# Query weights in two runs of 16 KB to a partition, with a second copy of x to match

## The chip, the cores and the metric

One core of one Trainium2 chip. The metric is device microseconds of one execution.

## The reference

One decode step: a layer norm of x (512 numbers), then two branches that are multiplied. Branch A is attention of 32 heads over the last 4,096 rows of a K and a V cache (64 MB, the bulk of the traffic); its query is `xn @ wq`, with `wq` 512 x 4,096 in bf16 (4 MB). Branch B is a small MLP on the same `xn`.

```
x  = A_x                                     # [1, 1, 512]
xn = layernorm(x)
q  = (xn @ wq) -> 32 heads of 128            # wq: 512 x 4096
s  = softmax(q k^T * Dh**-0.5) v @ wo        # k, v: the last 4096 of 32768 rows, 32 heads
x1 = xn + shifted(gelu(layernorm(xn) @ w1)) @ w2     # one row only, so the shifted rows are zero
g  = silu(x1 + gelu(layernorm(x1) @ w3) @ w4)
out = x + s * g
```

## The kernel before

x lies over the partitions four numbers to each (`x[4p + c]` in partition p), and the weights' rows lie the same way, so partition p of the query weights is one run of 4 rows, 32 KB, in memory. All large loads go through the sync engine's queue, in program order; the two small loads of x through the scalar engine's.

```python
    small.tile([P, 64], BF16, name="pad")                 # unused: places the tiles after it
    ...
    def load(dst, src):
        return tc.keep_in_program_order(nc.sync.dma_start(out=dst, in_=src))

    x_bf = small.tile([P, KC], BF16, name="x_bf")         # KC = 4: 128 pieces of 8 B
    nc.scalar.dma_start(out=x_bf[:], in_=A_x.rearrange("a b (p c) -> p (a b c)", p=P))
    x_row = small.tile([P, P], BF16, name="x_row")        # 4 rows of 256 B
    ...
    load(w2_sb[:], ...); load(w3_sb[:], ...); load(w4_sb[...], ...)   # 4096, 11008, 8192, 2048, 1024 B to a partition
    wq_sb = wts.tile([P, KC, HD], BF16, name="wq_sb")
    load(wq_sb[:], A_wq.rearrange("(p c) n -> p c n", p=P))           # 32,768 B to a partition
    ...
    x_f = small.tile([P, KC], FP32, name="x_f")
    nc.vector.tensor_copy(out=x_f[:], in_=x_bf[:])
    xc, negmean, rstd = ln_stats(x_f[:], "x")
    xn_f = small.tile([P, KC], FP32, name="xn_f")
    nc.vector.tensor_scalar(out=xn_f[:], in0=xc[:], scalar1=rstd[:], scalar2=None, op0=ALU.mult)
    xn_bf = small.tile([P, KC], BF16, name="xn_bf")
    nc.vector.tensor_copy(out=xn_bf[:], in_=xn_f[:])
    ...                                                   # the MLP branch, up to bv and g_row
    for h in range(H):
        for c in range(KC):
            nc.tensor.matmul(qT_ps[:, h:h + 1], lhsT=wq_sb[:, c, h * Dh:(h + 1) * Dh],
                             rhs=xn_bf[:, c:c + 1], start=(c == 0), stop=(c == KC - 1))
    ...                                                   # 16 steps of K (VectorE and TensorE) and V (TensorE)
```

K tiles have 6 buffers, V tiles 3, of 16 KB to a partition each; K and V loads are issued as buffers come free.

Of the kernel before, what the change touches and what calls it, by code (L numbers as in the profile page):

```python
# [8 lines left out]
P = 128  # L9
BF16 = mybir.dt.bfloat16  # L10
FP32 = mybir.dt.float32
ACT = mybir.ActivationFunctionType
ALU = mybir.AluOpType
# [16 lines left out]
def kernel(  # L30
# [14 lines left out]
    nc = tc.nc  # L45
# [20 lines left out]
    small = ctx.enter_context(tc.tile_pool(name="small", bufs=1))  # L66
# [3 lines left out]
    ps_o = ctx.enter_context(tc.tile_pool(name="ps_o", bufs=1, space=PSUM))  # L70
    ps_y = ctx.enter_context(tc.tile_pool(name="ps_y", bufs=1, space=PSUM))
    sm_pool = ctx.enter_context(tc.tile_pool(name="sm", bufs=3))
    small.tile([P, 64], BF16, name="pad")
    wts_guard = tc.tile_pool(name="wts", bufs=1)
    wts = wts_guard.__enter__()

    def load(dst, src):
        return tc.keep_in_program_order(nc.sync.dma_start(out=dst, in_=src))  # L78

    x_bf = small.tile([P, KC], BF16, name="x_bf")  # L80
    nc.scalar.dma_start(out=x_bf[:], in_=A_x.rearrange("a b (p c) -> p (a b c)", p=P))
    x_row = small.tile([P, P], BF16, name="x_row")
    nc.gpsimd.memset(x_row[:], 0.0)
    nc.scalar.dma_start(out=x_row[0:P:32, :], in_=A_x.rearrange("a b (j n) -> (a b j) n", j=KC))
# [6 lines left out]
    load(w4_sb[:, 8:10, :], B_w4[8 * P:10 * P, :].rearrange("(p c) n -> p c n", p=P))  # L91
    load(w4_sb[0:96, 10, :], B_w4[10 * P:F, :])
    wq_sb = wts.tile([P, KC, HD], BF16, name="wq_sb")
    load(wq_sb[:], A_wq.rearrange("(p c) n -> p c n", p=P))

    def load_kv(pool, cache, i, cuts=None):
        t = pool.tile([P, CP, Dh], BF16, tag="kv", name="kv")
# [57 lines left out]
    def ln_stats(src_f, tag):  # L155
        ps = ps_misc.tile([P, KC], FP32, tag="misc", name="ln_ps")
        nc.tensor.matmul(ps[:], lhsT=ones_f[:], rhs=src_f, start=True, stop=True)  # L157
        tot = small.tile([P, 1], FP32, name=f"ln_tot_{tag}")
        nc.vector.reduce_sum(out=tot[:], in_=ps[:], axis=AX.X)
        negmean = small.tile([P, 1], FP32, name=f"ln_negmean_{tag}")  # L160
        nc.vector.tensor_scalar(out=negmean[:], in0=tot[:], scalar1=-1.0 / D,
                                scalar2=None, op0=ALU.mult)
        xc = small.tile([P, KC], FP32, name=f"ln_xc_{tag}")
        nc.vector.tensor_scalar(out=xc[:], in0=src_f, scalar1=negmean[:], scalar2=None,
                                op0=ALU.add)
        sq = small.tile([P, KC], FP32, name=f"ln_sq_{tag}")
        nc.vector.tensor_tensor(out=sq[:], in0=xc[:], in1=xc[:], op=ALU.mult)
        ps2 = ps_misc.tile([P, KC], FP32, tag="misc", name="ln_ps2")
        nc.tensor.matmul(ps2[:], lhsT=ones_f[:], rhs=sq[:], start=True, stop=True)
        vtot = small.tile([P, 1], FP32, name=f"ln_vtot_{tag}")  # L170
        nc.vector.reduce_sum(out=vtot[:], in_=ps2[:], axis=AX.X)
        rstd = small.tile([P, 1], FP32, name=f"ln_rstd_{tag}")
        nc.vector.tensor_scalar(out=rstd[:], in0=vtot[:], scalar1=1.0 / D,
                                scalar2=LN_EPS, op0=ALU.mult, op1=ALU.add)
        nc.gpsimd.tensor_tensor(out=rstd[:], in0=rstd[:], in1=neg_half[:], op=ALU.pow)
        return xc, negmean, rstd
# [4 lines left out]
    xc, negmean, rstd = ln_stats(x_f[:], "x")  # L181
    xn_f = small.tile([P, KC], FP32, name="xn_f")
    nc.vector.tensor_scalar(out=xn_f[:], in0=xc[:], scalar1=rstd[:], scalar2=None, op0=ALU.mult)
    xn_bf = small.tile([P, KC], BF16, name="xn_bf")
    nc.vector.tensor_copy(out=xn_bf[:], in_=xn_f[:])



# [3 lines left out]
    for j in range(KC):  # L192
        for c in range(KC):
# [10 lines left out]
                            op0=ALU.add, op1=ALU.mult)  # L204
# [56 lines left out]
    for c in range(2):  # L261
        nc.vector.tensor_copy(
            out=few[:, c, 0:4 * NE].rearrange("p (a b) -> p a b", b=4),
            in_=ident_bf[:, 4 * NE * c:4 * NE * (c + 1)].rearrange("p (b a) -> p a b", b=4))
# [18 lines left out]
                            scalar1=two[:], scalar2=None, op0=ALU.add)  # L283
    md = const.tile([4, 2, 2], FP32, name="md")
    nc.vector.tensor_scalar(out=md[:], in0=ident_f[0:4, 2:4].unsqueeze(1).to_broadcast([4, 2, 2]),
                            scalar1=-1.0, scalar2=1e30, op0=ALU.add, op1=ALU.mult)
# [5 lines left out]
    for r in range(2):  # L292
        nc.vector.tensor_copy(out=pick_f[:, :, r, :],
                              in_=ident_bf[:, 32 * r:32 * r + 8].rearrange("p (i a) -> p i a", a=2))
# [351 lines left out]
```

## Time and profile before

| | |
|---|---|
| three timed executions | 195.66, 195.69, 195.76 us |
| the execution that was profiled | 196.92 us (span 195.1) |
| DMA traffic | 78.84 MB in the sync queue |
| stream | from 1.75 to 190.46 us of the span, never empty after 2.5 us |

The prediction shows the page's slices and the queue table. A packet is one record of a DMA engine moving one run of bytes; "stream" is used here for the run of packets in the sync engine's queue on the 16 DMA engines; as it is never empty, the kernel ends 4.6 us after it does.

### The profile page before, as it was taken

What the parts mean: (1) busy time and instruction counts of PE and PEld (TensorE: products, weight loads), DVE (VectorE), ACT (ScalarE), POOL (GpSimd) and SP (SyncE); (2) the same over time, 40 slices, a digit from 0 to 9 for tenths busy, and PEclk for the clock granted to TensorE, in tenths of its full rate; (3) what the DMA queues carried; (4) which work ended last, traced back from release to release, by engine and by line L of the source; (5) the groups of instructions that cost most, each with busy time, mean ns of one, the idle gap of its engine ahead of it and who ended that gap; (6) DMA issues with size and microseconds to landing.
All of it is one profiled execution on the core that took longest, in us unless ns stands there. A gap on an engine that the chain in (4) does not pass through costs nothing.

```text
span 195.1 us, 4727 instructions
## 1 busy us (share of the span) xinstructions
PE 137.3 (70%) x2108; PEld 105.2 (54%) x2108; DVE 145.2 (74%) x164; ACT 79.0 (40%) x173; POOL 6.3 (3%) x13
## 2 busy tenths in 40 slices
PE   0549779673785899397977957367767897957751
PEld 0434469563784945235967342167656536945640
DVE  0550109999999999999999999079899996982001
ACT  2003019881945742327467053152555018933000
POOL 2110007000000000000000000000000000000000
PEclk9999966967558559759687696965555569675555
DMA  6999999999999999999999999999999999999980
GB/s 200 413 415 410 373 427 423 428 420 430 430 423 430 430 425 427 433 430 430 423 430 430 427 433 427 430 433 430 430 430 427 430 422 432 423 433 420 402 311 4
DMA packets 7052, 79.13 MB, mean 406 GB/s; under 512 B 889, under 2 KB 1753, under 8 KB 2265
## 3 DMA queue, kind: packets, MB, share of 16 engines
q1 hardware_dynamic: 6880, 78.84, 96.1%
q8 instruction: 16, 0.26, 0.5%
q10 hardware_dynamic: 152, 0.00, 0.0%
q14 instruction: 4, 0.02, 0.0%
HBM read 78.84 MB, written 0.00 MB: 404 GB/s over the span
## 4 chain that ended last, share of the span: by engine, by line
DVE 47%; DMA 24%; PE 17%; ACT 5%; issue 4%; SPq 1%; POOL 1%; POOLq 0%
DVE S L315 28%; DVE prod L313 15%; DMA kv<-in_A_v_cache_dram 15%; DMA wo_rows<-in_A_wo_dram 7%; ACT kt L329 4%; PE yr_ps L507 3%; PE oT L442 3%; PE ov L431 3%; DMA x_bf<-in_A_x_dram 2%; PE qT_ps L239 2%; PE hr_ps L223 2%; SPq L78 1%; PE a_ps L212 1%; PE hr_ps L220 1%; DVE m L353 1%
## 5 line engine op out<-in xcount | busy, mean ns | idle before, releaser
L315 DVE TENSOR_REDUCE S<-prod 128x20 f32<-128x2560 bf16 (+1 forms) x32 | 83.8, 2620 | 1.1
L329 ACT COPY kt<-pt 128x1024 bf16<-128x1024 bf16 x54 | 50.9, 1021 | 28.0 <-PE pt L328 28.0
L313 DVE TENSOR_TENSOR prod<-kv,q_bc 128x2560 bf16<-128x2560 bf16 (+1 forms) x32 | 44.3, 1385 | 9.0 <-DMA kv<-in_A_k_cache_dram 6.4
L328 PE MATMUL pt<-ident_bf,kv 128*128 128x128 bf16 x432 | 41.0, 277 | 10.4 <-DMA kv<-in_A_k_cache_dram 8.8
L328 PEld LDWEIGHTS <-kv 128*128 128x128 bf16 x432 | 37.4, 129 | 13.7 <-DMA kv<-in_A_k_cache_dram 10.2
L334 PE MATMUL sT<-qT_bf,kt 128*128 128x2 bf16 x432 | 17.7, 165 | 11.8 <-ACT kt L329 11.2
L442 PE MATMUL oT<-pT,kv 128*128 128x2 bf16 x768 | 22.3, 165 | 4.6 <-DMA kv<-in_A_v_cache_dram 4.6
L442 PEld LDWEIGHTS <-kv 128*128 128x128 bf16 x768 | 21.4, 102 | 6.0 <-DMA kv<-in_A_v_cache_dram 5.9
L334 PEld LDWEIGHTS <-kt 128*128 128x128 bf16 x432 | 15.9, 102 | 14.8 <-ACT kt L329 14.0
L431 PE MATMUL ov<-kv,pT 128*8 128x512 bf16 x64 | 21.9, 517 | 0.0
L431 PEld LDWEIGHTS <-pT 128*8 128x8 bf16 x64 | 6.7, 109 | 13.9 <-issue 11.4
L378 ACT ACTIVATE pT<-S,mb 128x64 bf16<-128x64 f32 x32 | 10.9, 356 | 0.2
L371 PE MATMUL mb_ps<-md,par_t 4*128 4x4 f32 x16 | 3.9, 314 | 9.5 <-DVE md L363 9.5
L374 ACT COPY mb<-mb_ps 128x4 f32<-128x4 f32 x8 | 1.3, 162 | 19.3 <-PE mb_ps L371 19.3
L371 PEld LDWEIGHTS mb_ps<-md,par_t 4*128 4x128 f32 x16 | 3.4, 263 | 10.1 <-issue 8.8
L462 DVE TENSOR_TENSOR o<-oT,rden 128x2 bf16<-128x2 f32 x3 | 0.5, 160 | 11.1 <-PE oT L442 11.1
L466 ACT ACTIVATE o<-oT,rden 128x1 bf16<-128x1 f32 x26 | 4.7, 264 | 6.6 <-PE oT L449 4.7
L226 DVE COPY hr<-hr_ps 1x512 f32<-1x512 f32 x1 | 0.7, 677 | 7.9 <-PE hr_ps L223 7.9
L507 PE MATMUL yr_ps<-wo,ox 128*1 128x512 bf16 x16 | 6.3, 576 | 0.0
L378 ACT ACTIVATION_READ_ACCUMULATOR pT<-S,mb 128x1 f32 x32 | 6.0, 187 | 0.0
L157 PE MATMUL ln_ps<-x_f,ones_f 128*128 128x4 f32 x4 | 1.2, 364 | 6.1 <-DVE x_f L180 5.1
L215 ACT ACTIVATE a_bf<-a_ps 128x10 bf16<-128x10 f32 x1 | 0.2, 180 | 12.4 <-PE a_ps L212 12.4
(116 smaller groups left out, 95.1 us busy)
## 6 DMA issues: line engine op xcount, KB each, us to landing
kv<-in_A_k_cache_dram SPq DMA_DIRECT2D x16, 2048.0 KB, 29.9
kv<-in_A_v_cache_dram SPq DMA_DIRECT2D x15, 2048.0 KB, 26.9
wq_sb<-in_A_wq_dram SPq DMA_DIRECT2D x1, 4096.0 KB, 19.1
wo<-in_A_wo_dram SPq DMA_DIRECT2D x1, 2048.0 KB, 28.2
w_sb<-in_B_w_dram SPq DMA_DIRECT2D x1, 1376.0 KB, 6.7
w_sb<-in_B_w_dram SPq DMA_DIRECT2D x1, 1024.0 KB
wo<-in_A_wo_dram SPq DMA_DIRECT2D x1, 1024.0 KB, 26.8
kv<-in_A_v_cache_dram SPq DMA_DIRECT2D x1, 1024.0 KB
```

Of the source, the lines that this page charges most:

```text
L223: nc.tensor.matmul(hr_ps[:], lhsT=a_bf[0:m, i:i + 1], rhs=w4_sb[0:m, i, :], start=False, stop=(i == len(chunks) - 1))
L313: nc.vector.tensor_tensor(out=prod[:, 0:m, :], in0=kn[:, rows, :], in1=q_bc[:, s:s + 1, :].to_broadcast([P, m, Dh]), op=ALU.mult)
L315: nc.vector.tensor_reduce(out=st[s // 2]["S"][:, s % 2, rows], in_=prod[:, 0:m, :], axis=AX.X, op=ALU.add)
L328: nc.tensor.transpose(pt[:, i, :], kn[:, n + b + i, :], ident_bf[:])
L329: nc.scalar.copy(out=kts[s][:, b:b + w, :], in_=pt[:, 0:w, :])
L334: nc.tensor.matmul(st[s // 2]["sT"][:, s % 2, c, :], lhsT=kt[:, c, :], rhs=qT_bf[:, 2 * s:2 * s + 2], start=True, stop=True)
L371: nc.tensor.matmul(mb_ps[:], lhsT=par_t[:].rearrange("k b a -> k (b a)"), rhs=md[:].rearrange("k r a -> k (r a)"), start=True, stop=True)
L378: nc.scalar.activation(out=s["pT"][:, i // 2, :, i % 2], in_=s["S"][:, i // 2, :], func=ACT.Exp, scale=scale, bias=mb[:, i:i + 1], accum_o ...
L431: nc.tensor.matmul(s["ov"][32 * r:32 * r + 8], lhsT=s["pT"][:, r, c:c + 4, :].rearrange("p i a -> p (i a)"), rhs=v[:, c:c + 4, :], start=F ...
L442: nc.tensor.matmul(s["oT"][:, 2 * r:2 * r + 2], lhsT=v[:, c, :], rhs=s["pT"][:, r, c, :], start=(c == 0), stop=(c == CP - 1))
L466: nc.scalar.mul(o_blk[b][:, c + k:c + k + 1], st[g]["oT"][:, hl + k:hl + k + 1], st[g]["rden"][:, hl + k:hl + k + 1])
L507: nc.tensor.matmul(yr_ps[:], lhsT=ox_blk[i][:, t:t + 1], rhs=wo_blk[i][:, t, :], start=(t == 0), stop=(t == n - 1))
```

## The change

Its intent: runs of 16 KB, the size at which all K and V tiles stream, in place of the slower packets of 32 KB. Row `256 j + 2 p + i` of the query weights now goes to partition p, so x is needed in that order too, and a second copy of it is loaded; the layer norm's scaling is applied to that copy directly.

```diff
-    small.tile([P, 64], BF16, name="pad")
+    small.tile([P, 48], BF16, name="pad")
@@
     nc.scalar.dma_start(out=x_bf[:], in_=A_x.rearrange("a b (p c) -> p (a b c)", p=P))
+
+    x_q = small.tile([P, 2, 2], BF16, name="x_q")
+    nc.scalar.dma_start(out=x_q[:], in_=A_x.rearrange("a b (j p i) -> p (a b j) i", j=2, p=P))
     x_row = small.tile([P, P], BF16, name="x_row")
@@
-    load(wq_sb[:], A_wq.rearrange("(p c) n -> p c n", p=P))
+    load(wq_sb[:].rearrange("p (j i) n -> p j (i n)", j=2),
+         A_wq.rearrange("(j p i) n -> p j (i n)", j=2, p=P))
@@
-    nc.vector.tensor_copy(out=xn_bf[:], in_=xn_f[:])
+    nc.vector.tensor_scalar(out=xn_bf[:], in0=x_q[:].rearrange("p j i -> p (j i)"), scalar1=negmean[:],
+                            scalar2=rstd[:], op0=ALU.add, op1=ALU.mult)
```

## The prediction

> **What bounds the kernel now.** I read the page's slices first, then the queue table, then the chain that ended last, and then the trace in three places: a table of stretches, the timeline around the query projection, and the single packet records. The slices:
>
> ```profile
> DVE  0550109999999999999999999079899996982001
> ...
> DMA  6999999999999999999999999999999999999980
> GB/s 200 413 415 410 373 427 423 428 420 430 430 423 430 430 425 427 433 430 430 423 430 430 427 433 427 430 433 430 430 430 427 430 422 432 423 433 420 402 311 4
> ```
>
> A slice is 195.1 / 40 = 4.88 us. The DMA row is at 9 from the second slice to the thirty-eighth, and the rate below it is flat at 420 to 433 GB/s from the sixth slice on. Only the first five slices and the end are lower. The fifth (19.5 to 24.4 us, 373) holds the end of the query weights. The queue table says whose bytes these are:
>
> ```profile
> q1 hardware_dynamic: 6880, 78.84, 96.1%
> ...
> q10 hardware_dynamic: 152, 0.00, 0.0%
> ```
>
> Queue 1 is the sync engine's, with 78.84 MB, 96.1% of what 16 engines have in the span. Queue 10 is the scalar engine's: today's two small loads of x, 152 packets, no share worth printing. In stretches (columns: stretch, its length, busy us and count of PE, PEld, DVE, ACT, POOL, granted clock, DMA share, GB/s):
>
> ```profile
> 24.00:40.00 16.00, 12.40 (x242) 11.31 (x239) 10.86 (x8) 9.69 (x13) 3.50 (x1) 0.78 1.01 425
> 40.00:100.00 60.00, 45.20 (x615) 34.98 (x612) 59.11 (x49) 30.77 (x64) 0.00 (x0) 0.69 1.01 428
> 100.00:160.00 60.00, 44.50 (x568) 31.10 (x568) 53.30 (x41) 22.66 (x58) 0.00 (x0) 0.66 1.01 429
> 160.00:187.00 27.00, 19.77 (x472) 17.32 (x471) 14.15 (x24) 12.71 (x34) 0.00 (x0) 0.68 1.00 422
> ```
>
> The DMA share is 1.00 or 1.01 throughout. VectorE is as full, 59.11 of 60 us, from 40 to 100 us, but only 53.30 of 60 after that. The chain names VectorE for nearly half the span:
>
> ```profile
> DVE 47%; DMA 24%; PE 17%; ACT 5%; issue 4%; SPq 1%; POOL 1%; POOLq 0%
> ```
>
> That invites the reading "VectorE is the bound", so I checked who waits for whom where the two meet. The timeline of VectorE has this line:
>
> ```profile
> 127.95 1.49 DVE L313 TENSOR_TENSOR prod<-kv,q_bc 128x2560 bf16<-128x2560 bf16 x1 [5.55 <-DMA kv<-in_A_k_cache_dram]
> ```
>
> VectorE stands idle 5.55 us for a K tile. By then it has caught up with the loads, and whatever it had been late before is forgiven. The DMA queue is never forgiven: summing the bytes issued and the packets finished, I find that at every issue after the first the work already queued would last at least 3.0 us more, and at least 9.0 us from the first V tile on (11.8 us there at 30.03 us; 9.0 us at 173.83 us, the last V tile). **The bound is the DMA stream**, from its first packet at about 2.1 us to its last at 190.5 us, plus about 4.6 us of tail. A change is worth what it takes out of that stream.
>
> **What the Trainium skill says.** (1) "DMA: Bandwidth & Descriptors", section "Bandwidth": the fabric ceiling is 16 x 32 B x 850 MHz = 435 GB/s, and a large load was measured near it. The trace agrees, with 427 to 433 in the good slices. So no gain is to be had beyond bringing the query weights up to the rate of the others. (2) Same page, "Queues, rings and completion order": each DMA engine round-robins between the queues that it has work for, at packet granularity. The trace agrees: x's 8-byte packets lie singly between the 4,096-byte packets of w2, from 2.1 to 4.2 us. This matters for the new load of x. (3) Same page, "Why a DMA increments its semaphore by 16 and not by 1": one descriptor moves one contiguous run of the last dimension. The trace agrees: 128 packets of 8 B for x, 128 of 32,768 B for the query weights. So the changed loads are 256 packets of 4 B and 256 of 16,384 B. (4) Same page, "Latency and other measured facts": DMA copies whose partition pitch is a large power of two ran slower, with channel aliasing as an unverified inference. The pitches told there are 512 KiB and up; ours goes from 32 KiB to 16 KiB. It may or may not be the reason for what follows; no run here shows it.
>
> **The change part by part.**
>
> *The query weights.* In the packet records the 128 packets of 32,768 B take 1,360 ns in the mean (1,347 to 1,400), or 24.1 B/ns. The 4,096 packets of 16,384 B take 616 ns in the mean and 611 in the median, 26.6 to 26.8 B/ns. The shorter ones fit a line: 309 ns for 8,192 B and 611 for 16,384 B give 302 ns for each 8,192 B plus 7 ns for a packet. On that line 32,768 B would take 1,215 ns, so the long packet is 145 ns dearer than it should be. Each DMA engine has 128 / 16 = 8 of them: 8 x 1,360 = 10.9 us, and the records agree, from 10.5 or 11.1 to 22.0 us. After: 16 packets at 613 ns plus 2 ns of gap each = 9.84 us. **Saved: 1.0 us of the stream.** Evidence that this layout runs at 611: a block of output weights, also 16 KB runs one after another over the partitions, streams from 115.6 to 120.3 us at 611.6 ns a packet. The K tiles likewise alternate between two far regions, as the two halves will.
>
> *The second copy of x.* 256 / 16 = 16 packets of 4 B for each engine plus one semaphore write. Such packets show 9 ns, and between two 4,096-byte packets with one of them the gap was about 13 ns instead of 2. **Cost: 17 x 11 = 0.19 us of the stream.**
>
> *Its latency.* Because of the round robin, those 16 packets take turns with the weights. After x (done at 4.2 us) come 8 packets of w3 at 413 ns and 8 of w4 at 309 ns on each engine, so the copy completes only at about 10 us. The row form of x, issued after it, lands soon after that, where its packets ran at 5.7 to 6.1 before. On VectorE the cast now depends on the copy and moves ahead of the sum that feeds the second layer norm. These lines show when that order ran before:
>
> ```profile
> 8.60 0.23 DVE L183 TENSOR_SCALAR xn_f<-ln_xc_x,ln_rstd_x 128x4 f32<-128x4 f32 x1 [0.45 <-POOL ln_rstd_x L175]
> 8.73 0.34 DVE L203 TENSOR_SCALAR xn_row<-x_row,ln_negmean_x,ln_rstd_x 128x128 f32<-128x128 bf16 x1
> 8.99 0.17 DVE L185 CAST xn_bf<-xn_f 128x4 bf16<-128x4 f32 x1
> 9.06 0.15 DVE L197 TENSOR_TENSOR x_f<-xn_f,hs_ps 128x4 f32<-128x4 f32 x1
> ```
>
> So the sum moves from 9.06 to about 10.4 us, and all of the MLP branch with it. The projection stands behind that branch on PE, as its PSUM buffer is read by line 231 first:
>
> ```profile
> 22.58 0.29 DVE L231 TENSOR_TENSOR bv<-xn_row,h_ps 128x128 f32<-128x128 f32 x1 [0.66 <-PE h_ps L152]
> 22.92 3.34 PE L239 MATMUL qT_ps<-xn_bf,wq_sb 128*128 128x1 bf16 x128 [0.41 <-DVE bv L231]
> ```
>
> The query weights were there at 3.31 + 19.1 = 22.4 us, so today the branch ends 0.4 us after the load. I expect the branch 1 to 2 us later (fewer mask instructions now stand inside it, so not the whole 1.4 plus the wait for the row) and the load 0.8 us earlier. The projection then starts at 24 to 25 us, **1 to 2 us later although its weights are earlier**, and so does the first product on VectorE, 29.37 now. Off the path: the first V issue has 11.8 us of queued work before it, and VectorE's 5.55 us wait for K takes up its lateness.
>
> *Removed.* One VectorE cast of 170 ns, replaced by one of about 240 ns. Nothing on the stream.
>
> *Moved issues.* The eight DMA semaphores rotate over all loads, so with one load more the query weights wait for the first x (about 4.8 instead of 3.3 us), and the first K for the new copy (about 10 instead of 4.86). The weights have 7.8 us of queued work before them and the first K 17, so neither starves the stream.
>
> Sum: -1.04 + 0.19 = -0.85 us; 195.69 - 0.85 = **194.85 us**, 0.4%.
>
> **Rivals.** (a) *The late projection costs its delay*: VectorE is the bound, the chain's 47%, and the end moves by +1 to +2 us, to 196.7 to 197.7. For it: VectorE's row of nines from 29 to 118 us. Against: the 5.55 us wait at 122.4 to 127.95 and 9 us or more of queued work at every V and K issue. (b) *The small packets eat the gain*: if each of the 16 cost some 65 ns of its engine rather than 11, the sum is zero, 195.7. For it: 4,096-byte packets beside the small ones take 232 ns in the mean. Against: their median is 159, and the long ones are the very first, cold packets. (c) *The long packets are slow for their place and not for their length* (early in the kernel, beside nothing else), and 16 KB packets there are slow as well: then +0.2, 195.9. For it: the first K packets behind them, from 20 to 23 us, take 623 ns rather than 611. Against: w3 just ahead of them runs at 413 ns for 11,008 B, on the line. (d) *A tail effect*: at 187 to 190 us the engines finish unevenly (busy about 0.75), so the slowest decides; this can give or take 0.2 us.
>
> **Range and chances.** The three runs before lie within 0.1 us, and the stream's length is arithmetic on narrow packet times, so the range is narrow: (a) with 6%, (b) and (c) partly with 15% set the upper end at 195.6, and full rate with a good tail sets the lower at 194.4. A move of 2% is 3.9 us, four times all that the weights can give and twice the worst delay.
>
> **What would show each step.** Right: 256 packets of 16,384 B more at 611 to 620 ns, none of 32,768; the slices of 12 to 24 us at 425 or so; x's copy landing at about 10 us, seen as VectorE idle before the line that makes xn_bf; the projection later than 22.92 us, yet the last wo_rows landing near 189.9 us instead of 190.76. Wrong: stretches with a DMA share under 0.98 after 12 us (starved, rival a), or the wait for K at 128 us gone; 16 KB packets of the query weights over 660 ns (c); or long gaps around the 4-byte packets (b).

## The result

**196.78 us** (196.63 to 196.89, six executions), beside 195.72 us for the kernel before (195.66 to 195.93, six executions): slower by 0.5%. The ratio is 1.0052, with an interval of 1.0039 to 1.0065: clear of 1. 194.85 was forecast, in a range of 194.4 to 195.6.

Yet the two profiles show almost the same span, 195.1 before and 195.0 after. The page of the changed kernel, slices and queues:

```profile
DMA  6999999999999999999999999999999999999970
GB/s 200 334 420 437 433 430 417 420 425 430 427 433 430 430 428 430 427 430 433 430 427 433 427 430 430 430 430 427 427 430 423 430 422 432 418 439 422 407 296 3
...
q1 hardware_dynamic: 7008, 78.84, 95.8%
...
q10 hardware_dynamic: 424, 0.00, 0.1%
```

The slices from 9.8 to 24.4 us (third to fifth) have risen to 420 to 437, as hoped. But the second slice, 4.9 to 9.8 us, has fallen from 413 to 334 GB/s, while the scalar engine's queue went from 152 to 424 packets and still shows a share of only 0.1%. The timeline of VectorE and TensorE in the changed kernel has the lines that answer to those shown of before:

```profile
8.48 0.23 DVE L187 TENSOR_SCALAR xn_f<-ln_xc_x,ln_rstd_x 128x4 f32<-128x4 f32 x1 [0.45 <-POOL ln_rstd_x L179]
11.71 0.29 DVE L189 TENSOR_SCALAR xn_bf<-x_q,ln_negmean_x,ln_rstd_x 128x4 bf16<-128x4 bf16 x1 [2.99 <-DMA x_q<-in_A_x_dram]
11.90 0.15 DVE L202 TENSOR_TENSOR x_f<-xn_f,hs_ps 128x4 f32<-128x4 f32 x1
...
26.16 3.53 PE L244 MATMUL qT_ps<-xn_bf,wq_sb 128*128 128x1 bf16 x128 [0.41 <-DVE bv L236]
...
127.74 1.49 DVE L318 TENSOR_TENSOR prod<-kv,q_bc 128x2560 bf16<-128x2560 bf16 x1 [1.94 <-DMA kv<-in_A_k_cache_dram]
```

VectorE stands idle 2.99 us for the copy, which lands at 11.7 us, and the projection starts at 26.16 us instead of 22.92. VectorE still waits for K near 128 us, by 1.94 us. So two things are to be explained: the fallen second slice, and why equal spans go with times that differ by 1.06 us.

### The profile page after: what moved, and what is told of

It reads as the page before. It is cut to its first block, busy times and chain, and to the rows that moved or that the text cites. A ratio compares the mean times of both kernels' runs of the same rounds, so it can differ in the third digit from the quotient of the medians.

```text
span 195.0 us, 4729 instructions
## 1 busy us (share of the span) xinstructions
PE 135.7 (70%) x2108; PEld 104.2 (53%) x2108; DVE 145.6 (75%) x164; ACT 79.0 (41%) x173; POOL 6.3 (3%) x13
## 4 chain that ended last, share of the span: by engine, by line
DVE 47%; DMA 22%; PE 18%; issue 5%; ACT 5%; SPq 1%; POOL 1%; POOLq 0%
DVE S L320 28%; DVE prod L318 15%; DMA kv<-in_A_v_cache_dram 13%; DMA wo_rows<-in_A_wo_dram 7%; ACT kt L334 4%; PE yr_ps L512 3%; PE ov L436 3%; PE oT L447 3%; DMA x_bf<-in_A_x_dram 2%; PE hr_ps L228 2%; PE qT_ps L244 2%; PE a_ps L217 1%; SPq L78 1%; PE hr_ps L225 1%; DVE m L358 1%
## 5 line engine op out<-in xcount | busy, mean ns | idle before, releaser
L333 PE MATMUL pt<-ident_bf,kv 128*128 128x128 bf16 x432 | 40.4, 275 | 5.9 <-DMA kv<-in_A_k_cache_dram 4.3
L333 PEld LDWEIGHTS <-kv 128*128 128x128 bf16 x432 | 36.7, 128 | 9.2 <-DMA kv<-in_A_k_cache_dram 5.2
L447 PEld LDWEIGHTS <-kv 128*128 128x128 bf16 x768 | 21.4, 102 | 5.7 <-DMA kv<-in_A_v_cache_dram 5.7
L339 PEld LDWEIGHTS <-kt 128*128 128x128 bf16 x432 | 15.9, 102 | 13.5 <-ACT kt L334 12.6
L436 PE MATMUL ov<-kv,pT 128*8 128x512 bf16 x64 | 20.8, 496 | 0.0
L364 PE MATMUL mt_ps<-ident_f,m 128*2 128x128 f32 x8 | 2.8, 352 | 4.9 <-DVE m L358 4.9
## 6 DMA issues: line engine op xcount, KB each, us to landing
wo<-in_A_wo_dram SPq DMA_DIRECT2D x1, 2048.0 KB, 24.4
```

Source lines behind the costliest of these rows:

```text
L333: nc.tensor.transpose(pt[:, i, :], kn[:, n + b + i, :], ident_bf[:])
L339: nc.tensor.matmul(st[s // 2]["sT"][:, s % 2, c, :], lhsT=kt[:, c, :], rhs=qT_bf[:, 2 * s:2 * s + 2], start=True, stop=True)
L436: nc.tensor.matmul(s["ov"][32 * r:32 * r + 8], lhsT=s["pT"][:, r, c:c + 4, :].rearrange("p i a -> p (i a)"), rhs=v[:, c:c + 4, :], start=F ...
L447: nc.tensor.matmul(s["oT"][:, 2 * r:2 * r + 2], lhsT=v[:, c, :], rhs=s["pT"][:, r, c, :], start=(c == 0), stop=(c == CP - 1))
```

## The experiments

Sixteen runs in five batches. Times given are of single executions; "beside before" are executions of the kernel before on the same chip in the same batch. Where packet durations and ends of a part are told, they are from the traces' packet records; "MLP part" is the stream up to the last packet of w4. Each run has a short name (c1, e1 to e15). The edits of e4, e5, e12 and e13 are shown as they differ from e2, that of e15 as it differs from e12, those of e3 and e7 are made on the changed kernel, and the rest on the kernel before. Comments in them are added here, and "..." stands for what is left out. Where x_q was added to the kernel before (32 B with its padding; two in e4), the unused pad was made smaller by as much; e13's larger tile came without that.

### The control: the kernel before as its own rival (c1)

> The kernel before, unchanged, as a control. The profiled span of before is 195.1 us and that of the changed kernel 195.0, yet the timed medians are 195.72 and 196.78. Theory A (the loss is real, in runs that nobody profiles): ratio 1.000, time 195.7. Theory B (a kernel handed in as the new one is timed some 1.1 us higher than the one it is compared with, whatever it does): ratio about 1.0055, time 196.8.

Edit: none. Six executions: 195.72, 195.73, 195.86 and 196.87, 196.89, 197.30. Beside before: ten from 195.34 to 196.01, and one of 197.17. Neither theory A nor B holds as stated: **the kernel has two modes.** Over all batches the kernel before, this control and the profiled execution included, ran 62 times: 49 executions lie from 195.34 to 196.02, 13 from 196.67 to 198.12, and none between (two of the 13, 198.07 and 198.12, stand apart from the rest, which end at 197.30; nobody traced them). The control's trace (an execution of 195.86 us, in the faster mode, span 194.0) beside the one that the prediction was read from (196.92) shows what differs. The stretch from 12 to 20 us lies wholly within the query weights' load; columns as in the prediction, the last two being DMA share and GB/s. First the kernel before as it was first profiled, then the control:

```profile
12.00:20.00 8.00, 6.36 (x55) 3.76 (x55) 1.05 (x10) 1.52 (x3) 0.55 (x1) 1.00 0.99 381
```

```profile
12.00:20.00 8.00, 6.30 (x53) 3.66 (x53) 1.11 (x10) 1.52 (x3) 0.55 (x1) 1.00 1.01 438
```

The same instructions at 381 and at 438 GB/s. In the packet records, the 32,768-byte packets take 1,359 to 1,361 ns in one (113 of 128; the others 1,347 to 1,400), and 1,213 ns in the other (110 of 128; mean 1,226, with a slow start): 8 x (1,360 - 1,226) = 1.07 us for each DMA engine, the whole difference of the spans (195.05 - 193.98). And 1,213 is what the line through the smaller packets gives (1,215). The control's trace against that of the changed kernel, part by part:

| | control (faster mode) | changed kernel |
|---|---|---|
| end of the MLP part | 11.10 us | 12.06 us |
| from there to the end of the stream | 178.29 us | 178.28 us |
| span | 193.98 us | 195.03 us |

**All of the loss lies before 12.06 us, and the query weights' new layout gives nothing** against the mode in which the kernel before mostly runs. The stretch of the changed kernel:

```profile
12.00:20.00 8.00, 4.76 (x51) 3.96 (x52) 3.55 (x25) 1.27 (x3) 0.56 (x1) 1.00 1.00 428
```

From here on "faster mode" and "slower mode" are told apart by the times, or by the packets where there is a trace. The times alone can deceive: the changed kernel's 196.63 to 196.89 lie in or next to the band of the slower mode of the kernel before (from 196.67). It is the trace (196.81) that shows the changed kernel in the faster one, with the weights' packets at 611 ns and the MLP part late.

### Only the 16 KB packets (e1)

> The query weights as 16 KB packets with the layout of before: two loads of half the columns each, no second copy of x. Theory of the prediction (the long packets cost 1.0 us of the stream because of their length, and nothing is lost elsewhere): profiled span 194.1 us, packets of 16,384 B at 611 to 616 ns where those of 32,768 B took 1,360; against the control the time is 1.0 us less. Rival (the alternation of two far regions, or the adjacency of partitions, is what makes 16 KB packets fast): packets of 640 to 680 ns and no gain.

```diff
-    load(wq_sb[:], A_wq.rearrange("(p c) n -> p c n", p=P))
+    wq_src = A_wq.rearrange("(p c) n -> p c n", p=P)
+    load(wq_sb[:, 0:2, :], wq_src[:, 0:2, :])
+    load(wq_sb[:, 2:4, :], wq_src[:, 2:4, :])
```

195.76, 195.77, 195.78, 195.88, and 196.59, 196.91: no gain, and both modes. The trace (196.59) caught a change of mode in the middle of a load: packets of 611 ns up to some 13.5 us, then 681 ns until the weights end. So 16 KB packets have a slow mode as well, 681 / 611 = 1.11, like 1,359 / 1,213 = 1.12. The prediction's theory fails: what made its packets slow was not their length.

### Only the copy, loaded and not used (e2)

> The second copy of x is loaded, in its 4-byte packets, and not used; the query weights stay in 32 KB packets. Theory S (the small packets hold up the weights' packets beside them, 0.94 us of the stream as in the profile of the changed kernel): the end of the MLP weights at 12.0 us instead of 11.1, profiled span 196.0, 0.9 us over the control. Rival L (what costs is the late landing of the copy and the row, which delays the projection): the projection is late by some 2 us here too, as the row form of x lands late, and the span is then 0 or 2 us longer, but not by the stream's 0.9. Prediction's own figure: 0.2 us.

```diff
+    x_q = small.tile([P, 2, 2], BF16, name="x_q")
+    nc.scalar.dma_start(out=x_q[:], in_=A_x.rearrange("a b (j p i) -> p (a b j) i", j=2, p=P))
```

196.71, 196.73, 196.81, 196.81, 196.90, and one of 198.52. **The load of the copy alone makes the whole loss**, 1.1 us; 196.8 is the changed kernel's time. None of the six comes near 195.7. The trace is of the 198.52 execution (weights' packets at a third value, 1,435 ns), but its MLP part can be used: it ends at 12.09 us. The predicted 0.2 us for these packets was wrong by a factor of five.

### The copy through the sync queue (e3)

> The changed kernel, but the second copy of x goes through the sync queue, ahead of all the weights: its 16 packets per DMA engine then take no turns with the weights. Theory S: the weights' packets are back at 413 and 309 ns, the stream starts 0.2 to 0.4 us later and is 0.6 to 0.8 us shorter in all; span 194.3; the projection is not late. If each small packet costs its 59 ns wherever it stands, the span stays at 195.0.

```diff
-    nc.scalar.dma_start(out=x_q[:], in_=A_x.rearrange("a b (j p i) -> p (a b j) i", j=2, p=P))
+    load(x_q[:], A_x.rearrange("a b (j p i) -> p (a b j) i", j=2, p=P))
```

196.44, 196.54, 196.66, 196.76, and 197.38, 197.49. The weights' packets are back (w3 at 417 ns in the mean, w4 at 309), but the stream's first weight packet starts at 2.54 us and not at 1.75, and the MLP part ends at 11.60. Of these 0.8 us at the start, 0.5 are the copy's place in the sync engine's order: w2 is issued at 1.23 us and not at 0.73. The expectation of 0.6 to 0.8 us less than the changed kernel is missed: 0.2 less. Of the 0.9 us over the kernel before, 0.5 are in the MLP part; the rest was not traced, as this profile fell in the slower mode (the changed layout's packets at 681 ns).

### Twice and half the small packets (e4, e5)

> As e2 (copy loaded, not used, query weights as before), but the copy is loaded twice: 512 packets of 4 B, 32 for each DMA engine. The copy alone took the stream's MLP part from 11.10 to 12.09 us and the time from 195.7 to 196.8. Theory S (each small packet costs its engine some 60 ns when it takes turns with the weights): the MLP part ends near 13.0 us, time 197.7 in the faster of the two modes of the query weights (and 1.1 to 2 us more in the slower). If the cost is one for having a second queue active at all, or comes once: 12.1 us and 196.8.

```diff
+    x_q2 = small.tile([P, 2, 2], BF16, name="x_q2")
+    nc.scalar.dma_start(out=x_q2[:], in_=A_x.rearrange("a b (j p i) -> p (a b j) i", j=2, p=P))
```

e4: 196.98, 197.05, and 199.03, 199.60. The MLP part ends at 12.03 us. Double the packets cost 1.25 us in the faster mode and not 2. (The traced execution, 199.60, has the weights at 1,213 ns and 91 slow K and V packets of 16 KB, over 650 ns, where the control has 16; what disturbed it is not explained.)

> As e2, but the extra load has the layout of the first x: 128 packets of 8 B, 8 for each DMA engine. Theory S, cost by packet: half of e2's 1.0 us, MLP part ending near 11.6 us, time 196.2. If the bytes or the two-byte pairs mattered: the same as e2, 196.8.

```diff
-    nc.scalar.dma_start(out=x_q[:], in_=A_x.rearrange("a b (j p i) -> p (a b j) i", j=2, p=P))
+    nc.scalar.dma_start(out=x_q[:].rearrange("p j i -> p (j i)"), in_=A_x.rearrange("a b (p c) -> p (a b c)", p=P))
```

e5: 196.43, 196.51, 196.55, and 196.94. The first three cost 0.7 us. The trace is of the fourth: its weights run in the faster mode (1,213 ns), its MLP part ends at 12.06 us as late as in e2, and so half the packets cost 1.15 us there. **A fixed price for each small packet is refuted**: 8 more for each engine cost 0.7 or 1.15 us, 16 cost 1.1 and 32 cost 1.25.

### The copy, or all of x, without small packets (e6 to e9)

> The kernel before without its own small packets: x comes as one row of 1 KB and four matmuls with one row spread it over the partitions, in place of the 128 packets of 8 B; query weights as before. Theory S: these 8 packets for each engine cost some 0.5 us too (packets of w2 have a mean of 232 ns, median 159); without them w2 ends 0.4 to 0.5 us earlier, time 195.2 in the faster mode. Rival (the long packets of w2 are cold ones and nothing else, as the prediction had it): 195.7.

> The changed kernel with the second copy made by four matmuls from a row of 1 KB and not by 4-byte packets; the query weights in their two runs of 16 KB. If the copy's packets were all of the loss, and the new layout of the weights gains nothing against the faster mode of the old: 195.7 to 195.8, and 196.8 in executions where packets run at 681 ns. If the weights' new layout is worth what the prediction said (1.0 us against every execution): 194.8. If it costs something itself: above 195.9.

The first (e6) replaces the kernel's own 128 pieces of x by one row and four matmuls; the second (e7) keeps the changed kernel, and makes its second copy in that way. The edit of the first:

```diff
-    x_bf = small.tile([P, KC], BF16, name="x_bf")
-    nc.scalar.dma_start(out=x_bf[:], in_=A_x.rearrange("a b (p c) -> p (a b c)", p=P))
+    x_one = small.tile([1, D], BF16, name="x_one")
+    nc.scalar.dma_start(out=x_one[:], in_=A_x.rearrange("a b n -> (a b) n"))
@@
-    nc.vector.tensor_copy(out=x_f[:], in_=x_bf[:])
+    xs_ps = ps_misc.tile([P, KC], FP32, tag="misc", name="xs_ps")
+    for c in range(KC):
+        nc.tensor.matmul(xs_ps[:, c:c + 1], lhsT=x_one[0:1, c::4], rhs=ones_bf[0:1, 0:1], start=True, stop=True)
+    nc.vector.tensor_copy(out=x_f[:], in_=xs_ps[:])
```

Both missed: 196.88 to 197.27 (five) and 197.39 to 197.64 (four), above everything expected. The traces show why: packets of the whole kernel are a little slower. Of the K and V packets only a fifth still take 611 ns (790 of some 4,100; in the control 3,481), most take 613 to 621; those of 8,192 B take 313 in the median and not 309. The new tile had moved all later tiles in on-chip memory by 1,024 - 32 = 992 B. The pad of the kernel before is there for this, and I had not minded it. With the pad 32 B larger:

> As e6 (no small packets at all), with the unused pad enlarged by 32 B so that every later tile in on-chip memory stands where it stood before, up to a multiple of 1 KB. In e6 and e7 the packets of the whole kernel took 4 to 10 ns more (611 became 614 and 621, 309 became 313 and 321); both had shifted the tiles by 992 B. If that shift is why: packets back at 611 and 309, time 195.6 in the faster mode (w2 has 0.3 us less of packet time, of which e6 showed 0.1 us in the stream), and 196.7 in the slower. If the tile of x in one row is why: 197.0 again.

> As e7 (the changed kernel with its second copy made on TensorE), pad corrected in the same way. If the copy's small packets are the whole loss and the weights' new layout gains nothing over the faster mode of the old: 195.7, or 196.8 where packets lock at 681 ns. If the new layout is worth the predicted 1.0 us: 194.8.

The first (e8) ran in 195.18, 195.26, 195.36, and 196.24. **In the faster mode it is 0.4 us faster than the kernel before**, whose faster mode on that chip was 195.60 to 195.94; its packets are back at 611 and 309 ns, and its MLP part ends at 10.75 us instead of 11.10 (at 10.74 in e14, the same kernel). The kernel's first load of x had cost 0.35 us of the stream too.

The second (e9) is the changed kernel without the small packets of its copy: 195.73, 195.84, 195.84, 196.04, and 196.79, 196.98. That is the kernel before, in both its modes. **Without the copy's packets the loss is gone, and nothing is gained.** Its stretch in the faster mode stands beside 438 of the control:

```profile
12.00:20.00 8.00, 6.20 (x54) 4.03 (x55) 1.37 (x12) 1.52 (x3) 0.55 (x1) 1.00 1.02 436
```

### The copy late, and the projection late (e10, e11)

> As e2 (the copy is loaded in its 4-byte packets and not used), but issued only after the activation of the MLP, near 16 us, so that it takes turns with the 32 KB packets of the query weights and the 16 KB packets of K and not with w3 and w4. In e2 the stream ran at 262 to 366 GB/s from 4.5 to 9 us and at 400 to 420 after, with small packets in both. If each small packet costs some 60 ns wherever it takes its turn: 196.7. If it is the early stretch alone: 195.7, and the slices after 16 us at their usual rate.

```diff
     nc.scalar.activation(out=a_bf[0:96, 10:11], in_=a_ps[0:96, 10:11], func=ACT.Gelu_apprx_tanh)
+    nc.scalar.copy(out=x_q[:].rearrange("p j i -> p (j i)"), in_=a_bf[:, 0:4])   # holds the load back
+    nc.scalar.dma_start(out=x_q[:], in_=A_x.rearrange("a b (j p i) -> p (a b j) i", j=2, p=P))
```

e10: 196.62, 196.90, 196.96, and 197.47; the mode of the three that were not traced is unknown. In the trace (196.62, weights in the faster mode, 0.9 us over the control in the span) the MLP part and the weights are untouched, the small packets run from 20 us on, and the stream falls to between 288 and 409 GB/s from 22 to 26.5 us, against the K packets of 16 KB. So the cost is not tied to the early stretch. But from 20 to 22 us, and after 26.5, small packets take their turns at 409 to 427 GB/s.

> The kernel before, with some 4 us of idle work put on VectorE ahead of the layer norm's result, so that the projection starts near 26.5 us as in the changed kernel, and nothing in the loads is touched. If the bound is the stream: 195.7, span 193.9 to 194.0 where the packets of the query weights take 1,213 ns, with a shorter wait for K near 128 us. Rival a of the prediction (VectorE is the bound): 198 to 199.5.

```diff
+    hold = prod_pool.tile([P, 20, Dh], BF16, tag="prod", name="hold")
+    nc.vector.tensor_scalar(out=hold[:], in0=zero_bf[:].unsqueeze(1).to_broadcast([P, 20, Dh]), scalar1=rstd[:], ...)
+    held = sm_pool.tile([P, 2, CP - 32], FP32, tag="own", bufs=1, name="held")
+    nc.vector.tensor_reduce(out=held[:, 0, 0:20], in_=hold[:], axis=AX.X, op=ALU.add)      # zeros
-    nc.vector.tensor_scalar(out=xn_f[:], in0=xc[:], scalar1=rstd[:], scalar2=None, op0=ALU.mult)
+    nc.vector.scalar_tensor_tensor(out=xn_f[:], in0=xc[:], scalar=rstd[:], in1=held[:, 0, 0:KC], ...)
```

e11: 195.60, 195.86, and 197.06, 198.00, beside before in the same two groups. The traced execution has a span of 193.9, no longer than the control's, with these lines, first those of the control:

```profile
23.88 3.50 PE L239 MATMUL qT_ps<-xn_bf,wq_sb 128*128 128x1 bf16 x128 [0.41 <-DVE bv L231]
...
126.51 1.49 DVE L313 TENSOR_TENSOR prod<-kv,q_bc 128x2560 bf16<-128x2560 bf16 x1 [3.07 <-DMA kv<-in_A_k_cache_dram]
```

```profile
27.87 3.48 PE L245 MATMUL qT_ps<-xn_bf,wq_sb 128*128 128x1 bf16 x128 [0.41 <-DVE bv L237]
...
127.32 1.49 DVE L319 TENSOR_TENSOR prod<-kv,q_bc 128x2560 bf16<-128x2560 bf16 x1
```

**A projection 4 us later than the control's costs nothing** (the changed kernel's came 2.3 us later). VectorE is not the bound. It has little more to give, though: its wait for K near 127 us, 3.07 us in the control, is gone here.

### What makes the small packets dear (e12, e13, e15)

> As e2 (256 packets of 4 B, loaded early and not used), but the 256 sources are 1 KB apart in another tensor, not side by side within the 1 KB of x. If the cost is the engines crowding on one spot of memory: 195.7 in the faster mode, MLP part ending at 11.1 us. If it is the packets themselves: as e2, 196.8, 12.1 us.

```diff
-    nc.scalar.dma_start(out=x_q[:], in_=A_x.rearrange("a b (j p i) -> p (a b j) i", j=2, p=P))
+    nc.scalar.dma_start(out=x_q[:], in_=A_wo[0:2 * P, 0:2].rearrange("(p j) i -> p j i", p=P))
```

e12: 195.55, 195.68, 195.72, 195.79, and the MLP part ends at 11.10 us as in the control: **256 packets of 4 B, with the sources 1 KB apart, cost nothing.** The view of the DMA queues from 4.5 to 9 us, first for the copy of x alone (e2), then for this run:

```profile
DMA packets 316, 1.46 MB, mean 324 GB/s; under 512 B 173, under 2 KB 173, under 8 KB 173
...
q10 hardware_dynamic: 157, 0.00, 1.8%
```

```profile
DMA packets 373, 1.85 MB, mean 411 GB/s; under 512 B 183, under 2 KB 183, under 8 KB 183
...
q10 hardware_dynamic: 167, 0.00, 2.1%
```

As many small packets in the scalar queue, with as little of the engines' time in the records, and 324 GB/s in the one, 411 in the other. What the small packets cost is mostly not in their own records: it is in longer packets of the weights beside them and in gaps. Up to the end of the MLP part, each DMA engine spends 8.69 us in the weights' packets in the control, 9.25 in e2 and 8.71 in e12; in the scalar queue's own packets it spends 0.09, 0.23 and 0.24. So of the 0.99 us by which e2 is late, 0.56 are longer packets, 0.15 the small packets themselves, and the rest gaps.

> As e12, but each of the 256 packets carries 512 B to its place (131 KB in all, by the line of 302 ns for 8,192 B some 16 x 26 = 0.42 us for each engine). If packets below 512 B are dear for their size: 196.1, MLP part ending near 11.6 us, cheaper than the 4-byte ones although they carry 128 times the bytes. If a second queue taking turns is dear whatever it carries: 197.1 or more, 12.4 us.

```diff
+    nc.scalar.dma_start(out=x_q[:], in_=A_wo[0:2 * P, 0:256].rearrange("(p j) i -> p j i", p=P))   # x_q: [P, 2, 256]
```

e13: 195.83, 195.89, 196.01, and 197.18 (traced: weights at 1,357 ns). 0.2 us over the kernel before, for 131 KB more, which are 0.3 us of the stream at 427 GB/s; the MLP part ends at 11.46 us. Here a second queue that takes turns costs about its bytes and no more.

> As e12, with the same tensor as source and the same 256 packets of 4 B, but all sources side by side in one row of 1 KB of that tensor, in the order of e2. e12 (sources 1 KB apart) cost nothing: 195.55 to 195.79. If the crowding of all sources in 1 KB is the cause: as e2, 196.7 to 196.9 in the faster mode, 12.1 us for the end of the MLP part, 320 to 350 GB/s from 4.5 to 9 us. If it was the place of x, or its being read three times: 195.7 and 11.1 us.

```diff
-    nc.scalar.dma_start(out=x_q[:], in_=A_wo[0:2 * P, 0:2].rearrange("(p j) i -> p j i", p=P))
+    nc.scalar.dma_start(out=x_q[:], in_=A_wo[0:1, :].rearrange("a (j p i) -> p (a j) i", j=2, p=P))
```

e15: 196.09, 196.11, 196.19, 196.24: crowded into one row of 1 KB of the same tensor, they cost again, 0.45 us, with the MLP part ending at 11.55. The rate of the stream by half microseconds, summed from the packet records (GB/s, at the time in us at the head of each column):

```
                    4.5  5.0  5.5  6.0  6.5  7.0  7.5  8.0  8.5  9.0  9.5 10.0
control             423  422  416  410  428  414  410  426  428  427  420  405
copy of x (e2)      366  363  329  327  291  360  354  262  343  402  417  421
spread (e12)        397  419  416  411  422  415  414  421  420  412  406  395
one row of wo (e15) 404  422  415  418  424  410  410  407  387  332  318  299
```

So where the sources lie makes the cost (e12 against e15, one tensor). Crowding is the likely reason, but it is not the only difference: e12's sources all have the same offset within a 1 KB row, those of e2 and e15 run through all offsets, and **no run separates crowding from offset**. (Were each small read to fetch up to 512 B around it, that would not be enough: e13 fetched as much for each packet and cost 0.2 us.) When and for how long it strikes differs too: 4.5 us for x, 2 us and later for a row of wo. Why it strikes within such a stretch and not for as long as small packets run **stays open**; so the counts of e4 and e5 stay unexplained too.

### The better version again (e14)

> e8 once more for its interval: no small packets, pad corrected. e8's three executions in the faster mode took 195.18, 195.26 and 195.36, beside 195.60 to 195.94 of the kernel before. Expected: 195.2 to 195.4 in the faster mode, ratio of equal modes 0.9975, and 196.3 in the slower.

The kernel of e8: 195.14, 195.40, 195.40, 195.74, and 196.32, 196.46. Beside before: eight executions from 195.58 to 195.94, and 196.95, 197.23, 198.12. Means of the faster modes with e8's batch: seven executions of 195.35, against fifteen of 195.72 (195.58 to 195.94): 0.19% less. The ratio over all its runs, both modes mixed, is 0.9975 with an interval of 0.9931 to 1.002. So it beats both kernels mode for mode, by 0.37 us (the kernel before) and some 1.4 us (the changed one, from other batches), and the interval that mixes the modes does not settle it.

## Why the prediction was wrong

- **"The bound is the DMA stream": right.** The control and the changed kernel differ by 0.95 us in the end of the stream and by 1.04 in the span. The late projection cost nothing (e11). Rival (a) gave 196.7 to 197.7 us, and the measured 196.78 lies in it by luck: not the late projection made the loss.
- **"Saved: 1.0 us of the stream": the first step that failed.** The arithmetic on the 1,360 ns packets was right, but for the one execution that was profiled; in 49 of 62 executions of the kernel before it cannot have held, as their times are those of the control's 1,213 to 1,226 ns. Against these the gain is 0.0 (178.29 against 178.28 us). Both warnings were at hand: the profiled execution took 196.92 us and the timed ones 195.66 to 195.76, a gap of the very size of the gain I saw; and the line through the shorter packets gave 1,215. I took the departure from the line for a property of the length. Nor is the new layout free of it: its packets ran at 681 ns in e3 (the over 660 ns of rival c, but not in every execution), and e9 has two slow executions of six. That the changed kernel's six show no slow one is too few to tell.
- **"Cost: 17 x 11 = 0.19 us": the second, and the one that turned the sign.** It measured 0.96 us at the end of the MLP part and 1.06 in the time. The step multiplied the small packets' own records by their number; most of the cost lies in the packets beside them and in gaps (0.56 and 0.28 us of 0.99 in e2). Rival (b) named it, near the right size (65 ns for each small packet; 0.96 us are 60 for each of 16), and I argued it away. Its evidence, 232 ns in the mean for w2's packets, was weak by itself: e14, without small packets, still has 223. The slow ones tell more: 19 and 24 of w2's 128 packets over 300 ns in the kernel before and its control, 6, 9 and 12 in e6, e8 and e14. So first packets alone, as I had it, do not make them all. Without x's small packets w2 ended at 4.0 to 4.1 us instead of 4.3 to 4.4 in the kernel before and its control, and the MLP part 0.35 us earlier (e8).
- **The latency: right in kind, short in size.** The copy landed at 11.7 us, not at about 10, since the stream that it took turns with had slowed; the projection came 3.2 us later than in the trace that I read (2.3 later than in the control), not 1 to 2.
- **The moved issues: right in effect, wrong in one place.** The query weights were issued at 4.75 us as forecast, but it was the second K load that waited for the copy (11.70 us instead of 5.57), not the first (5.19 instead of 4.86). The stream was never empty.
- **Signs of being right that came true without the gain:** packets of 16,384 B at 611 ns, the slices at 420 to 437, the late projection. Only the stream's end told: forecast 0.85 us earlier than in the profile of before, it came 0.12 us earlier (190.34 against 190.46 us). One mean was misread: 616 ns for the 16,384-byte packets takes in 16 packets of another queue, and is 614 without them.
- **The range** had no room for a loss, because (a) was given 6%, and rivals (b) and (c), given 15%, stopped at 195.7 and 195.9; that small packets cost as much while the weights gain nothing was in none of them.

## What to carry to other kernels

Before building on a profile, compare the time of the profiled execution with the timed ones: where they differ by as much as the gain in view, the profile shows a mode and not the kernel. A load in pieces of a few bytes out of one small array has to be priced by what the stream beside it loses, not by its own records (1.1 us against 0.15 in e2); here one row and four matmuls did the same work at no cost that the times show. When a tile is added or removed, keep the later tiles' places, or an experiment measures the shift.

## What the Trainium skill lacked or had wrong

- "DMA: Bandwidth & Descriptors", "Why small descriptors are slow": it prices small descriptors by their own overhead. Missing is that 256 reads of 4 B out of one 1 KB slow the other queue's large packets: 324 GB/s instead of 411 over 4.5 us (e2, e12), 1.1 us in the time, and 0.0 with the sources 1 KB apart.
- The same page's Specifications table names 512 B as the smallest transfer for line rate and says that smaller ones do read-modify-write. In e12, 4-byte writes cost nothing that could be measured, so size alone was not the price here.
- "DMA: Bandwidth & Descriptors", "Latency and other measured facts", has slow power-of-two row pitches from 512 KiB up. No page has that one and the same load runs at 1,213, 1,359 or 1,435 ns a packet (611 or 681 for 16 KB) from execution to execution, mostly constant after its first packets, and changing in the middle of the load in e1 (611 to 681) and e8 (1,359 to 1,213). Pitches here were 16 and 32 KB; what selects the mode is open.
- "SBUF — State Buffer", "Operand start alignment", speaks of legality and says that its runs timed nothing. Here a shift of 992 B in the tiles' places took packets from 611 to 613 to 621 ns and cost 1.7 us in the whole kernel (lowest times, e6 196.88 against e8 195.18, where only the pad differs; the two ran on different chips, with the kernel before at 195.65 to 195.87 and 195.60 to 195.94 in its faster mode). Nearest to it is "DMA: Bandwidth & Descriptors", "How a descriptor splits into AXI transactions", by which a read that starts off a 256-byte boundary costs extra beats; it has no times, and here it was the written side that moved. Which boundary counts was not tested.
